# A long convolution and a linear attention in one kernel: paired tail rows, no row of ones, thirds of k, v and q, and a new order

## The chip, the cores and the metric

The kernel runs on one core of a Trainium2 chip. The metric is the device time of one execution in microseconds. Its instructions go to TensorE (matrix products, PE in the profile), VectorE (DVE), ScalarE (ACT), GpSimd (POOL) and SyncE (SP, which issues nearly all DMAs).

## The reference

Two independent computations share the program; their results stand side by side in the output. S = 2048 rows, D = 576 channels, bf16.

```python
# A: a short convolution, a product, a long convolution over the rows, a gate
k_shift = sum(k_pad[:, t:t+S, :] * shift_k[:, 3-t] for t in range(4))
kv = k_shift * v
y = irfft(rfft(pad(kv)) * rfft(pad(ssm_k)))[:, :S] + kv * ssm_D
a = q * y
# B: linear attention, 32 heads of 18 channels
q, k, v = split(x @ wqkv)
phi = lambda t: where(t > 0, t + 1, exp(t)) + 1e-6
kv = einsum("bhsd,bhse->bhde", phi(k), v); z = phi(k).sum(rows)
o = (phi(q) @ kv) / (phi(q) . z + 1e-6)
b = o @ wo
return concatenate([a, b], -1)
```

## The kernel before, in words

A program of some 690 operations is first described (each with the engines it may run on, what it reads and writes) and then issued in one order written out by hand, the text `PLAN`: a letter for the engine (P TensorE, D VectorE, A ScalarE, G GpSimd, S SyncE) and the number of the operation. `PLACES` gives each buffer its address or its PSUM bank. Each engine works through its own operations in that order; semaphores hold an operation until what it reads is there and the buffer that it writes is free. Operations marked `two=1` on GpSimd also wait for the last such operation of VectorE that stands ahead of them in the order, so that products of the two engines run one after the other.

Part A, for three chunks of 192 channels (`CC`):

- `kv_load` loads k (with three rows ahead of each stretch) and v in two halves of 8 rows per partition, all 576 channels in a row. `conv_piece` makes the four taps of a chunk and a half in one product of 6144 columns (`tap`, L423), adds them (`tap+`, once as an accumulating DMA, `acc`, for two of the six pieces) and multiplies by v (`tapv`).
- `h_piece` loads the long filter (`hs`), transposes it on TensorE (`htr`) into hT (`hev`).
- `s1` multiplies by a table (`Gsb`), from hT for the filter (Ch) and from v for the signal (Cu); `s2` transposes in 32 by 32 blocks on VectorE (`tr`, L527) and multiplies by 32 by 32 blocks on TensorE (L538), which gives the spectra sph and spu.
- `inv` multiplies the spectra (`p1`, `p2`, after an exchange X by DMA) and transforms back in part (V; sums `vs` and differences `vd` of its halves); `inv2` does the rest and multiplies by q (`yq`, `i2q`), and `yo` stores.

Part B:

- x comes by DMA, transposed by DMA for three of its four groups of 512 rows (`xT`, `xTt`) and on TensorE for the first (`xtr`, `xev`). 576 is four tiles of 128 rows and one of 64; this last tile is filled up to 128 with rows that meet zeros in the weights and one row of ones (`x4`, `w0`, `w1`, `xo`). The row of ones in x meets a row of ones in the weights and so adds 1 to each product.
- `kproj` (L663): for each of 16 blocks of 128 rows, ten products of 288 columns, then exp(u − 1) on ScalarE (`ek`, L668) and max(min(exp, 1), u) on VectorE (L671), u being the product with 1 added. EPS comes later.
- `qproj` (L685): for each of four groups the query channels in five chunks (`HCH`: four of 126 and one of 72), two, two and one at a time, five products of 512 columns to a chunk, the same phi (L688, L691) into pqT.
- `b_G` (L714) multiplies x by phi(k), with a column of EPS in pk whose result, `gcol`, is added when G is evacuated. From G come kv and z; `den`, `rden` and a pass through memory (`rw`, `rr`) give each query its reciprocal; before that product (`pqn`, L246) a pass on VectorE adds EPS to pqT (`pqe`, L823), and the denominators get their EPS part from 20 products of one column (L785, `dcol`). `b_out` (L860) multiplies by M (kv times wo) and stores.

Many operations pass through helpers: `tt` (L246, products and sums), `copy` (L233 on ScalarE, L235 on VectorE, L237 on GpSimd), `dma` (L226).

Of the kernel before, what the change touches and what calls it, by code (L numbers as in the profile page):

```python
# [16 lines left out]
HALF = 288  # L17
KT = [128, 128, 128, 128, 128]
# [8 lines left out]
EP, WX = True, False  # L27
# [91 lines left out]
def _tables():  # L119
# [69 lines left out]
def kernel(  # L189
# [57 lines left out]

    def psb(banks, name):
        return P.buf(name, [128, banks, 512], FP32, space="ps", banks=banks)
# [16 lines left out]
    wk = SB("wk", [128, 5, D], side=1)  # L266
    wq = SB("wq", [128, 5, D], side=1)
# [3 lines left out]
    pk = [SB("pk%d" % g, [128, 4, D + 1], side=1) for g in range(4)]  # L271
# [10 lines left out]
    hmask = lambda: cs(32, 640).rearrange("p (c m) -> p c m", c=5)  # L282
    maskbd = lambda: cs(672, 126)
    epsc = lambda: cs(798, 1)

    P.op("G", lambda e: nc.gpsimd.memset(neg1.t[:], -1.0), wr=[neg1], name="neg1", ms=1)
    for wx in (wk, wq):
        P.op("G", lambda e, wx=wx: nc.gpsimd.memset(wx.t[0:64, 4, :], 0.0), wr=[(wx, "o")], name="w0", ms=576)
        P.op("G", lambda e, wx=wx: nc.gpsimd.memset(wx.t[0:1, 4, :], 1.0), wr=[(wx, "o")], name="w1", ms=576)
    for g in range(4):  # L290
        P.op("G", lambda e, g=g: nc.gpsimd.memset(x4[g].t[:, :, 0:64], 1.0), wr=[(x4[g], "o")], name="x1", ms=256, st="x1%d" % g)
        P.op("G", lambda e, g=g: nc.gpsimd.memset(pk[g].t[:, :, D:D + 1], EPS), wr=[(pk[g], "e")], name="pke", ms=16, st="pke%d" % g)
    if not EP:
        for f in range(2):
            P.op("G", lambda e, f=f: nc.gpsimd.memset(pqT[f].t[64:128, 4, :], 0.0), wr=[(pqT[f], (4, g)) for g in (2 * f, 2 * f + 1)] + [(pqT[f], "r")], name="pqz", ms=1024, st="pqz%d" % f)
# [4 lines left out]
    load("cst", cst, lambda e: dma(e, cst.t[:], C_d), 256 * Ct.shape[1], 1612)  # L300
# [26 lines left out]
    def x_pairs(g):  # L327
# [8 lines left out]
        for p in range(2):  # L336
            for t0, tn in ((0, 4), (4, 1)):
                ps = psb(1, "xps")

                def tr(e, t0=t0, tn=tn, ps=ps, p=p):  # L340
                    o = ps.t.rearrange("p b c -> p (b c)").bitcast(BF)
                    for j in range(tn):
                        for i in range(2):
                            nc.tensor.transpose(out=o[:, 256 * j + 128 * i:256 * j + 128 * i + 128],
                                                in_=x4[g].t[:, 2 * p + i, :] if t0 == 4 else x_sb[g].t[:, 2 * p + i, 128 * j:128 * j + 128],
                                                identity=ident())
# [4 lines left out]
                P.op("P", tr, rd=[(x4[g], ("m", p)), (x4[g], "o"), idw] if t0 == 4 else [(x_sb[g], p), idw], wr=[ps], name="xtr",  # L351
# [3 lines left out]
    def xt_load(g):  # L355
# [9 lines left out]
        if g in XD:  # L365
# [4 lines left out]
            P.op("G", lambda e: nc.gpsimd.memset(b.t[0:1, 4, :], 1.0), rd=[(b, 4)], wr=[(b, 4)], name="xo", ms=512)  # L370
            return

    def wload(which, key):
        c0 = which * D
        wx = wk if which else wq
        load("wqk" + key, wx, lambda e: dma(e, wx.t[:, 0:4, :], ap(wqkv, c0, [[3 * D, 128], [3 * D * 128, 4], [1, D]])),
             589824, 1152, wr=[(wx, "m")], engs=EARLY)
        load("wqkt" + key, wx, lambda e: dma(e, wx.t[64:128, 4, :], wqkv[512:576, c0:c0 + D]), 73728, 1152,
             wr=[(wx, "t")], engs=EARLY)
# [32 lines left out]
    def conv_piece(cc, bh):
        kh, vt = khs[bh], vs[bh]
# [11 lines left out]
        P.op("D", tap, rd=[kh, (Wj, cc)], wr=[(m, 0), (m, 2)], name="tap",  # L425
# [5 lines left out]
        else:  # L431
# [4 lines left out]
        P.op("DG", lambda e: tt(e, vt.t[:, :, c0:c0 + CC], m.t[:, 0], vt.t[:, :, c0:c0 + CC], ALU.mult),  # L436
             rd=[(m, 0), (vt, "v")], wr=[(vt, cc)], name="tapv", n=1536, x2=1, two=1, st=st)
# [38 lines left out]
    def s1(cc, nm):  # L476
        dt = nm == "h" and cc in HDT
        C = SB("C" + nm, [128, CC // 4, 4, 32] if dt else [128, CC // 2, 32, 2])
        for ri in range(2):
            for bg in range(4):  # L480
                ps = psb(2, "s1ps")

                def mm(e, ri=ri, bg=bg, ps=ps):
                    for j in range(4):
                        b = 4 * bg + j
                        src = hT[cc].t[:, b, :] if nm == "h" else vs[bg // 2].t[:, b % 8, CC * cc:CC * cc + CC]
# [12 lines left out]
                rdk = [(vs[bg // 2], cc)] if nm == "u" else [(hT[cc], (i, bg // 2)) for i in range(5) if HP[i] < CC * cc + CC and HP[i + 1] > CC * cc]  # L499
# [7 lines left out]
    def s2(C, cc, pp, nm):  # L507
# [38 lines left out]
        if nm == "h":  # L546
# [55 lines left out]
    def inv2(gi):  # L602
# [4 lines left out]
        nb = 512 // n  # L607
        for bg in range(16 // nb):
# [11 lines left out]
            if ya:  # L620
# [5 lines left out]
                def mul2(e, bg=bg, yb=yb):  # L626
                    qs = qb.t[:, nb * (bg - 1):nb * (bg + 1), c0:c0 + n]
                    return tt(e, qs, yb.t[:], qs, ALU.mult)
                if bg % 2:
                    P.op("DG", mul2, rd=[yb, (qb, "q")], wr=[(qb, (gi, bg - 1)), (qb, (gi, bg))], name="yq", n=2 * nb * n, x2=1, two=1, st=st)  # L630
            elif bg % 2:
# [3 lines left out]
                def mul1(e, bg=bg, yb=yb):  # L635
                    qs = qb.t[:, nb * bg:nb * bg + nb, c0:c0 + n]
                    return tt(e, qs, yb.t[:], qs, ALU.mult)
                P.op("DG", mul1, rd=[yb, (qb, "q")], wr=[(qb, (gi, bg))], name="yq", n=nb * n, x2=1, two=1, st=st)
            else:
                def mul(e, bg=bg, yv=yv):  # L640
                    qs = qb.t[:, nb * bg:nb * bg + nb, c0:c0 + n]
                    tt(e, qs, yv(), qs, ALU.mult)
                P.op("D", mul, rd=[ps, (qb, "q")], wr=[(qb, (gi, bg))], name="i2q", n=nb * n, st=st)
            ns = max(nb, 4) if ya or gi not in YA else nb
            if (bg + 1) * nb % ns == 0:
# [3 lines left out]
                    qb.t[:, b4:b4 + ns, c0:c0 + n]), 256 * ns * n, 2 * n,  # L649
                     rd=[(qb, (gi, kk)) for kk in range(b4 // nb, (b4 + ns) // nb)], wr=[])  # L650
# [3 lines left out]
    def kproj(r):  # L654
        ps = psb(2, "kps")
        eb = SB("ek", [128, 2, HALF])
# [3 lines left out]
        def mm(e):  # L660
            for hh in range(2):
                for t in range(5):
                    nc.tensor.matmul(ps.t[:, hh, 0:HALF],  # L663
                                     lhsT=cols(xT.t[0:KT[t], t, :], r),
                                     rhs=wk.t[0:KT[t], t, HALF * hh:HALF * hh + HALF],
                                     start=(t == 0), stop=(t == 4))
        P.op("P", mm, rd=[wk] + ([xT] if r // 4 in XD else [(xT, (r % 4 // 2, t0)) for t0 in (0, 4)]), wr=[ps], name="k", mm=[(288, 128, 128)] * 10, st=st)
        P.op("A", lambda e: nc.scalar.activation(  # L668
            out=eb.t[:], in_=ps.t[:, :, 0:HALF], func=ACTF.Exp, bias=neg1.t[:]), rd=[ps, neg1], wr=[eb], name="kexp",
             n=576, st=st)  # L670
        P.op("D", lambda e: nc.vector.scalar_tensor_tensor(  # L671
            out=pk[r // 4].t[:, r % 4, 0:D].rearrange("p (h c) -> p h c", h=2), in0=eb.t[:], scalar=1.0,
            in1=ps.t[:, :, 0:HALF], op0=ALU.min, op1=ALU.max), rd=[ps, eb, (pk[r // 4], "e")], wr=[(pk[r // 4], r)], name="kphi", n=576, st=st)

    def qproj(c0, m, g):
# [6 lines left out]
        def mm(e):  # L682
            for c in range(c0, c0 + m):
                for t in range(5):
                    nc.tensor.matmul(ps.t[0:hn, c - c0, :], lhsT=wq.t[0:KT[t], t, HCH[c][0]:HCH[c][0] + hn], rhs=xT.t[0:KT[t], t, :],  # L685
# [308 lines left out]
```

## Time and profile before

| | |
|---|---|
| runs | 161.87, 162.35, 163.82 us; median 162.35 |
| profiled execution | 160.18 us; its span in the profile 158.4 us |
| TensorE busy | 143.7 us (91%) |
| VectorE busy | 141.2 us (89%) |
| ScalarE busy | 128.4 us (81%) |
| GpSimd busy | 55.6 us (35%) |
| DMA | 34.21 MB in 26237 packets, 15786 of them under 512 B |

The profile is of one execution. Busy time of TensorE is the time in which at least one product is under way. A row of a group reads: line, engine, operation, what is written from what, shapes, count, then busy us and the mean ns of one, then the engine's idle time just before them and what ended it. A stretch row gives for each engine busy us and the count of its instructions. Timeline rows are start, length, engine, line, operation.

### The profile page before, as it was taken

Reading aid. Unit: us, or ns where it says so; the run is one execution under the profiler, and the core shown is the slowest. Engines: PE = TensorE matmul, PEld = TensorE weight load, DVE = VectorE, ACT = ScalarE, POOL = GpSimd, SP = SyncE. Lnnn points to the kernel's source line nnn. Section 1 sums busy time; section 2 is a strip of 40 time slices with the busy share of each in tenths; the row PEclk is TensorE's granted clock in tenths of the full one; section 3 lists DMA queues with packets and bytes.
Section 4 is the critical chain, followed back from the end, with each engine's and each line's share of the span. In section 5 each row is a group of like instructions: output and inputs, shape, how many; then the busy total and the mean of one; then the engine's idle time right before and its main releaser. Section 6 shows DMA issues by size and latency. Waiting matters only on the chain.

```text
span 158.4 us, 4045 instructions
## 1 busy us (share of the span) xinstructions
PE 143.7 (91%) x1653; PEld 110.8 (70%) x1653; DVE 141.2 (89%) x161; ACT 128.4 (81%) x181; POOL 55.6 (35%) x48
## 2 busy tenths in 40 slices
PE   6799899999999999999999996877999999989860
PEld 2479676567785789677888885545567788889750
DVE  1245999999999999998999969999999999999980
ACT  3048889989977957744789999799999999998860
POOL 8300310012555789037903553999300000004020
PEclk9999999999999999999999999999999999999998
DMA  4999199999804997179337982799468707952975
GB/s 116 341 405 305 10 244 276 334 199 320 183 0 138 347 262 311 31 270 176 90 107 183 255 209 91 274 333 357 126 271 304 263 2 261 390 177 78 258 198 143
DMA packets 26237, 34.21 MB, mean 216 GB/s; under 512 B 15786, under 2 KB 20907, under 8 KB 25450
## 3 DMA queue, kind: packets, MB, share of 16 engines
q1 hardware_dynamic: 25674, 32.37, 65.4%
q0 software_dynamic: 544, 1.57, 5.5%
q8 instruction: 13, 0.21, 0.6%
q14 instruction: 6, 0.05, 0.1%
HBM read 20.70 MB, written 4.99 MB: 162 GB/s over the span
## 4 chain that ended last, share of the span: by engine, by line
DVE 43%; PE 26%; DMA 16%; issue 6%; ACT 6%; SPq 1%; DVEq 0%; ACTq 0%
PE ps_all L685 8%; PE ps_all L663 7%; DMA m<-m 7%; DVE X L246 6%; DMA kh<-in_A_k_dram 5%; DVE sph L246 5%; DVE m L423 4%; PE ps_all L714 4%; DVE ct L527 4%; DMA wk<-in_B_wqkv_dram 4%; DVE V L246 3%; DVE spu L235 3%; DVE m L246 3%; DVE VS L246 3%; PE ps_all L488 3%
## 5 line engine op out<-in xcount | busy, mean ns | idle before, releaser
L685 PE MATMUL ps_all<-xT,wq 128*126 128x512 bf16 (+1 forms) x100 | 23.4, 379 | 0.4 <-DVE pqT L691 0.2
L860 PE MATMUL ps_all<-M,pqT 126*128 126x288 bf16 (+1 forms) x160 | 21.9, 286 | 1.4 <-ACT M L233 0.7
L663 PE MATMUL ps_all<-wk,xT 128*128 128x288 bf16 x160 | 21.1, 286 | 0.8 <-DMA wk<-in_B_wqkv_dram 0.8
L246 POOL TENSOR_TENSOR pqT<-pqT,rb 126x1024 bf16<-126x1024 bf16 (+1 forms) x9 | 18.9, 2129 | 7.6 <-DVE pqT L823 4.2
L860 PEld LDWEIGHTS <-pqT 126*128 126x128 bf16 (+1 forms) x160 | 17.1, 110 | 4.9 <-issue 1.6
L233 ACT ACTIVATE Cu<-ps_all 128x768 bf16<-128x768 f32 x23 | 18.7, 856 | 2.1 <-DVE den L796 0.9
L423 DVE TENSOR_TENSOR m<-kh,Wj 128x6144 bf16<-128x6144 bf16 x6 | 20.0, 3351 | 0.0
L663 PEld LDWEIGHTS <-xT 128*128 128x128 bf16 x160 | 17.2, 110 | 3.9 <-DVE xT L235 0.8
L488 PEld LDWEIGHTS <-Gsb 128*128 128x128 bf16 x192 | 16.0, 97 | 4.8 <-issue 2.3
L233 ACT ACTIVATE Ch<-ps_all 128x768 bf16<-128x768 f32 x19 | 15.4, 845 | 4.2 <-PE ps_all L488 4.0
L233 ACT ACTIVATE V<-ps_all 128x1024 bf16<-128x1024 f32 x18 | 18.1, 1103 | 0.4 <-PE ps_all L576 0.4
L685 PEld LDWEIGHTS <-wq 128*126 128x126 bf16 (+1 forms) x100 | 12.8, 131 | 7.8 <-issue 1.1
L233 ACT ACTIVATE sph<-ps_all 128x1024 bf16<-128x1024 f32 x16 | 16.0, 1032 | 2.2 <-PE ps_all L538 2.2
L246 POOL TENSOR_TENSOR m<-m 128x3072 bf16<-128x3072 bf16 (+1 forms) x3 | 15.1, 5049 | 6.8 <-ACT eq L688 5.4
L714 PE MATMUL ps_all<-pk,x_sb 128*128 128x288 bf16 (+1 forms) x128 | 17.1, 286 | 0.0
L668 ACT ACTIVATE ek<-ps_all,neg 128x576 bf16<-128x576 f32 x16 | 11.9, 742 | 5.1 <-PE ps_all L663 4.7
L246 POOL TENSOR_TENSOR q<-yb,q 128x768 bf16<-128x768 bf16 (+1 forms) x2 | 2.5, 1275 | 36.8 <-DVE V L246 30.5
L714 PEld LDWEIGHTS <-x_sb 128*128 128x128 bf16 x128 | 12.3, 98 | 2.9
L233 ACT ACTIVATE spu<-ps_all 128x1024 bf16<-128x1024 f32 x14 | 14.1, 1090 | 0.0
L671 DVE SCALAR_TENSOR_TENSOR pk<-ek,ps_all 128x576 bf16<-128x576 bf16 x16 | 11.7, 750 | 1.9 <-ACT ek L668 1.9
L688 ACT ACTIVATE eq<-ps_all,neg 126x1024 bf16<-126x1024 f32 (+1 forms) x12 | 11.6, 972 | 2.1 <-PE ps_all L685 2.1
L691 DVE SCALAR_TENSOR_TENSOR pqT<-eq,ps_all 126x1024 bf16<-126x1024 bf16 (+1 forms) x12 | 12.0, 1027 | 0.0
(88 smaller groups left out, 294.5 us busy)
## 6 DMA issues: line engine op xcount, KB each, us to landing
X<-sph SPq DMA_DIRECT2D x18, 256.0 KB
v<-in_A_v_dram SPq DMA_DIRECT2D x2, 1152.0 KB
out_dram<-ob SPq DMA_DIRECT2D x16, 144.0 KB
q<-in_A_q_dram SPq DMA_DIRECT2D x1, 2304.0 KB
out_dram<-q SPq DMA_DIRECT2D x11, 192.0 KB
rb<-r_scr SPq DMA_DIRECT2D x8, 252.0 KB
x_sb<-in_B_x_dram SPq DMA_DIRECT2D x3, 576.0 KB
kh<-in_A_k_dram SPq DMA_DIRECT2D x1, 1584.0 KB
```

The costliest lines, as they stand in the source:

```text
L233: nc.scalar.activation(out=o, in_=i, func=ACTF.Copy)
L246: return (nc.vector if e == "DVE" else nc.gpsimd).tensor_tensor(out=o, in0=a, in1=b, op=op)
L423: return nc.vector.tensor_tensor(out=m.t[:], in0=i0, in1=i1, op=ALU.mult)
L488: nc.tensor.matmul(ps.t[:, bank, lo - 384 * bank:hi - 384 * bank], lhsT=Gsb.t[:, b, ri, :], rhs=src[:, lo - CC * j:hi - CC * j], start=Tru ...
L663: nc.tensor.matmul(ps.t[:, hh, 0:HALF], lhsT=cols(xT.t[0:KT[t], t, :], r), rhs=wk.t[0:KT[t], t, HALF * hh:HALF * hh + HALF], start=(t == 0 ...
L668: P.op("A", lambda e: nc.scalar.activation(out=eb.t[:], in_=ps.t[:, :, 0:HALF], func=ACTF.Exp, bias=neg1.t[:]), rd=[ps, neg1], wr=[eb], na ...
L671: P.op("D", lambda e: nc.vector.scalar_tensor_tensor(out=pk[r // 4].t[:, r % 4, 0:D].rearrange("p (h c) -> p h c", h=2), in0=eb.t[:], scal ...
L685: nc.tensor.matmul(ps.t[0:hn, c - c0, :], lhsT=wq.t[0:KT[t], t, HCH[c][0]:HCH[c][0] + hn], rhs=xT.t[0:KT[t], t, :], start=(t == 0), stop=( ...
L688: P.op("A", lambda e: nc.scalar.activation(out=eb.t[0:hn], in_=ps.t[0:hn], func=ACTF.Exp, bias=neg1.t[0:hn, :]), rd=[ps, neg1], wr=[eb], n ...
L691: P.op("D", lambda e: nc.vector.scalar_tensor_tensor(out=pqT[g // 2].t[0:hn, c0:c0 + m, 512 * (g % 2):512 * (g % 2) + 512], in0=eb.t[0:hn] ...
L714: nc.tensor.matmul(ps.t[0:m, 0, 0:n], lhsT=x4[r // 4].t[:, r % 4, :] if t == 4 else x_sb[r // 4].t[:, r % 4, 128 * t:128 * t + 128], rhs=p ...
L860: nc.tensor.matmul(ps.t[:, hh - h, 0:HALF], lhsT=cols(pqT[r // 8].t[0:128 if c == 4 and not EP else hn, c, 512 * (r // 4 % 2):512 * (r // ...
```

## The change

- **Tails in pairs.** The last tile of x's rows is held twice, on partitions 0 to 63 and 64 to 127. `kproj` does eight products over four full tiles and then one tail product for each half of its columns, the first on partitions 0 to 63, the second on 64 to 127, into two PSUM banks. `qproj` does the same for its two chunks.
- **No row of ones.** exp(u) is taken without a bias; a new operation (`kmin`, `qmin`: `cap1`, on GpSimd or VectorE) makes min(exp, 1) + EPS; phi is max(u + 1 + EPS, that). The passes that add EPS to pqT, the EPS column of pk, gcol, dcol and its 20 products, and the memsets of w0 and w1 go.
- **Last query columns with the keys.** The last 72 query channels are computed by `kproj` as its first 72 columns (324 columns a half for 288, `KH`), and `qtail` transposes them from pk on TensorE (four transposes a group) and copies them into pqT. The fifth chunk of `qproj` goes.
- **k, v, q by 192 channels.** Each chunk of 192 channels has its own k, v and q tile, loaded in pieces of 8 rows per partition; a row in memory is then 384 bytes.
- **New order.** `PLAN` and `PLACES` are written anew. It begins with the filter (hs, htr, s1 for Ch) and has the key blocks after it. Of the 24 new caps 16 are on GpSimd and 8 on VectorE. The additions of taps that were GpSimd's (two long, one short) are VectorE's, five more of the products with the reciprocal too; five sums and differences of V are GpSimd's; two more evacuations of spectra, two of xT and, net, two of yb are ScalarE's, as are the four copies of the transposed query columns.

```diff
+QT = 72
+KH = 324
...
+    def cap1(e, t):
+        return (nc.vector if e == "DVE" else nc.gpsimd).tensor_scalar(out=t, in0=t, scalar1=1.0, scalar2=EPS, op0=ALU.min, op1=ALU.add)
...
-            P.op("G", lambda e: nc.gpsimd.memset(b.t[0:1, 4, :], 1.0), rd=[(b, 4)], wr=[(b, 4)], name="xo", ms=512)
+            P.op("GDA", lambda e: copy(e, b.t[0:64, 4, :], b.t[64:128, 4, :]), rd=[(b, 4)], wr=[(b, 4)], name="xo", n=512)
...
+        kh = SB("kh%d" % cc, [128, 19, CC])
+        vt = SB("v%d" % cc, [128, 16, CC])
...
+        for bh in range(2):
+            load("kh", kh, lambda e, bh=bh: dma(e, kh.t[:, 3 + 8 * bh:11 + 8 * bh, :], ap(k, 8 * bh * D + c0, [[16 * D, 128], [D, 8], [1, CC]])),
+                 2048 * CC, 2 * CC, wr=[(kh, "m%d" % bh)])
...
         def mm(e):
             for hh in range(2):
-                for t in range(5):
-                    nc.tensor.matmul(ps.t[:, hh, 0:HALF],
-                                     lhsT=cols(xT.t[0:KT[t], t, :], r),
-                                     rhs=wk.t[0:KT[t], t, HALF * hh:HALF * hh + HALF],
-                                     start=(t == 0), stop=(t == 4))
+                for t in range(4):
+                    nc.tensor.matmul(ps.t[:, hh, 0:KH], lhsT=cols(xT.t[:, t, :], r),
+                                     rhs=wk.t[:, t, KH * hh:KH * hh + KH], start=(t == 0), stop=False)
+            for hh in range(2):
+                h = slice(64 * hh, 64 * hh + 64)
+                nc.tensor.matmul(ps.t[:, hh, 0:KH], lhsT=cols(xT.t[h, 4, :], r), rhs=wk.t[h, 4, 0:KH], start=False, stop=True)
...
-            out=eb.t[:], in_=ps.t[:, :, 0:HALF], func=ACTF.Exp, bias=neg1.t[:]), rd=[ps, neg1], wr=[eb], name="kexp",
-             n=576, st=st)
+            out=eb.t[:], in_=ps.t[:, :, 0:KH], func=ACTF.Exp), rd=[ps], wr=[eb], name="kexp", n=2 * KH, st=st)
+        P.op("GD", lambda e: cap1(e, eb.t[:]), rd=[eb], wr=[eb], name="kmin", n=2 * KH, two=1, st=st)
         P.op("D", lambda e: nc.vector.scalar_tensor_tensor(
-            out=pk[r // 4].t[:, r % 4, 0:D].rearrange("p (h c) -> p h c", h=2), in0=eb.t[:], scalar=1.0,
-            in1=ps.t[:, :, 0:HALF], op0=ALU.min, op1=ALU.max), rd=[ps, eb, (pk[r // 4], "e")], wr=[(pk[r // 4], r)], name="kphi", n=576, st=st)
+            out=pk[r // 4].t[:, r % 4, 0:2 * KH].rearrange("p (h c) -> p h c", h=2), in0=ps.t[:, :, 0:KH], scalar=1.0 + EPS,
+            in1=eb.t[:], op0=ALU.add, op1=ALU.max), rd=[ps, eb], wr=[(pk[r // 4], r)], name="kphi", n=2 * KH, st=st)
...
+    def qtail(g):
...
+            for a in range(4):
+                nc.tensor.transpose(out=o[0:QT, 128 * a:128 * a + 128], in_=pk[g].t[:, a, 0:QT], identity=ident())
...
+        P.op("DA", ev, rd=[ps], wr=[(pqT[g // 2], (4, g))], name="qtev", n=512, st=st)
...
-                P.op("D", lambda e, c=c, hn=hn, f=f: nc.vector.tensor_scalar(
-                    out=pqT[f].t[0:hn, c, :], in0=pqT[f].t[0:hn, c, :], scalar1=EPS, scalar2=None, op0=ALU.add),
-                     wr=[(pqT[f], (c, g)) for g in (2 * f, 2 * f + 1)], name="pqe", n=1024, two=1)
```

More of the change, by code (lines that the diff above doesn't have):

```diff
@@ L270 @@
     x4 = [SB("x4%d" % g, [128, 4, 128], side=1) for g in range(4)]
-    pk = [SB("pk%d" % g, [128, 4, D + 1], side=1) for g in range(4)]
+    pk = [SB("pk%d" % g, [128, 4, 2 * KH], side=1) for g in range(4)]
     pqT = [SB("pqT%d" % f, [128, 5, 1024], side=1) for f in range(2)]
@@ L688, in qproj @@
+            for c in range(c0, c0 + m):
+                h = slice(64 * (c - c0), 64 * (c - c0) + 64)
+                nc.tensor.matmul(ps.t[0:hn, c - c0, :], lhsT=wq.t[h, 4, HCH[c][0]:HCH[c][0] + hn], rhs=xT.t[h, 4, :], start=False, stop=True)
+        P.op("P", mm, rd=[xT, wq], wr=[ps], name="q", mm=[(512, 128, 126)] * (4 * m + 1), st=st)
         P.op("A", lambda e: nc.scalar.activation(
-            out=eb.t[0:hn], in_=ps.t[0:hn], func=ACTF.Exp, bias=neg1.t[0:hn, :]), rd=[ps, neg1], wr=[eb],
+            out=eb.t[0:hn], in_=ps.t[0:hn], func=ACTF.Exp), rd=[ps], wr=[eb],
@@ L690, in qproj @@
              name="qexp", n=512 * m, st=st)
+        P.op("GD", lambda e: cap1(e, eb.t[0:hn]), rd=[eb], wr=[eb], name="qmin", n=512 * m, two=1, st=st)
         P.op("D", lambda e: nc.vector.scalar_tensor_tensor(
-            out=pqT[g // 2].t[0:hn, c0:c0 + m, 512 * (g % 2):512 * (g % 2) + 512], in0=eb.t[0:hn],
-            scalar=1.0, in1=ps.t[0:hn], op0=ALU.min, op1=ALU.max), rd=[ps, eb], wr=[(pqT[g // 2], (c, g)) for c in range(c0, c0 + m)], name="qphi",
+            out=pqT[g // 2].t[0:hn, c0:c0 + m, 512 * (g % 2):512 * (g % 2) + 512], in0=ps.t[0:hn],
+            scalar=1.0 + EPS, in1=eb.t[0:hn], op0=ALU.add, op1=ALU.max), rd=[ps, eb], wr=[(pqT[g // 2], (c, g)) for c in range(c0, c0 + m)], name="qphi",
@@ L698 @@
     for g in range(4):
-        for c, m in ((0, 2), (2, 2), (4, 1)) if MQ else [(c, 1) for c in range(5)]:
-            qproj(c, m, g)
+        for c in (0, 2):
+            qproj(c, 2, g)
+        qtail(g)
     GT = SB("GT", [128, 5, D])
-    gcol = SB("gcol", [128, 5], FP32)
     def b_G(t):
```

273 lines of the change are left out of this document (120 added, 153 removed), and 29 rows, old and new, of the table PLACES.

## The prediction

> **What bounds the kernel now.** First the span, then the stretch view in three pieces (columns: matmul, weight loads, VectorE, ScalarE, GpSimd, each busy us with its count; then clock, DMA share, GB/s).
>
> ```profile
> span 158.4 us, 4045 instructions
> ...
> 0.00:20.00 20.00, 17.01 (x149) 12.48 (x150) 9.65 (x17) 10.43 (x16) 6.10 (x20) 1.00 0.71 233
> 20.00:150.00 130.00, 123.92 (x1474) 95.69 (x1472) 127.38 (x137) 115.40 (x159) 48.59 (x27) 1.00 0.72 216
> 150.00:158.40 8.40, 2.81 (x32) 2.59 (x32) 4.13 (x10) 2.59 (x7) 0.91 (x1) 0.92 0.64 177
> ```
>
> In the 130 us of the middle VectorE idles 2.6, TensorE 6.1, ScalarE 14.6. So two engines bound it together, VectorE first; 10.3 us of VectorE idleness lie in the first 20. A gain must come off VectorE, must not return on TensorE, or must come from the start. Counts below come from numbering the operations in both written-out orders.
>
> **TensorE.** The timeline of its matmuls (start, length, what); starts alone give the pace.
>
> ```profile
> 34.30 0.43 PE L538 MATMUL ps_all<-ct,idw 32*32 32x512 bf16 x16
> 34.66 1.41 PE L663 MATMUL ps_all<-wk,xT 128*128 128x288 bf16 x10
> 35.91 2.32 PE L685 MATMUL ps_all<-xT,wq 128*126 128x512 bf16 x10
> 38.07 1.39 PE L663 MATMUL ps_all<-wk,xT 128*128 128x288 bf16 x10
> 39.30 1.14 PE L457 MATMUL ps_all<-idw,hs 96*128 96x96 bf16 x16
> 40.27 1.39 PE L663 MATMUL ps_all<-wk,xT 128*128 128x288 bf16 x10
> 41.59 0.50 PE L538 MATMUL ps_all<-ct,idw 32*32 32x512 bf16 x16
> 42.02 2.37 PE L685 MATMUL ps_all<-xT,wq 128*126 128x512 bf16 x10
> ```
>
> A key product block takes 1.25 and 1.23 us, say 1.24 for ten of 288 columns, 0.431 ns a column. A query block takes 2.16, or 0.216 for each 512 columns. Sixteen 32-row products of 512 columns take 0.36 and 0.43 from their start to the next one's: they run side by side, so two tails in the two halves of the array should too. But the excursion costs more than one product's 0.216: 0.14 in the first case; in the second 0.21, and the key block ahead of it is 0.08 slower (1.32), 0.29 in all. Call this s, 0 to 0.29 for an excursion into half rows, and take 0.2, near the middle of the two shown.
>
> - Keys: 8 products and a pair, 9 × 324 × 0.431 = 1.255 us, plus s: 16 × (1.255 + 0.2 − 1.24) = +3.4.
> - Queries by two chunks: 9 × 0.216 + 0.2 against 2.16, eight times: −0.1.
> - The four last-chunk products go: 4 × 5 × 0.216 = −4.3.
> - Sixteen transposes of these query columns come, at 0.97 / 16 = 0.061 from the row at 39.30: +1.0.
>
> The sum is 0.0; −4.8 with s = 0, +2.2 with s = 0.29. Were the pairs to run in turn, 16 × 0.14 + 8 × 0.216 = 4.0 more.
>
> **VectorE.** Groups by operation (count, then busy us and mean ns of one).
>
> ```profile
> L823 DVE TENSOR_SCALAR pqT<-pqT 126x1024 bf16<-126x1024 bf16 (+1 forms) x10 | 3.8, 423 | 0.0
> L691 DVE SCALAR_TENSOR_TENSOR pqT<-eq,ps_all 126x1024 bf16<-126x1024 bf16 x8 | 9.4, 1207 | 0.0
> L691 DVE SCALAR_TENSOR_TENSOR pqT<-eq,ps_all 72x512 bf16<-72x512 bf16 x4 | 2.7, 666 | 0.0
> L671 DVE SCALAR_TENSOR_TENSOR pk<-ek,ps_all 128x576 bf16<-128x576 bf16 x16 | 11.7, 750 | 1.9 <-ACT ek L668 1.9
> L246 DVE TENSOR_TENSOR V<-V 128x896 bf16<-128x896 bf16 x9 | 5.5, 623 | 0.2
> L235 DVE CAST spu<-ps_all 128x1024 bf16<-128x1024 f32 x4 | 4.8, 1198 | 0.0
> L235 DVE COPY xT<-ps_all 128x1024 bf16<-128x1024 bf16 (+1 forms) x3 | 1.7, 558 | 4.2 <-PE ps_all L344 4.2
> L235 DVE CAST yb<-ps_all 128x384 bf16<-128x384 f32 x4 | 2.0, 548 | 0.0
> L246 DVE TENSOR_TENSOR m<-m 128x3072 bf16<-128x3072 bf16 x2 | 3.5, 1756 | 0.0
> L246 DVE TENSOR_TENSOR m<-m 128x1536 bf16<-128x1536 bf16 x5 | 4.9, 977 | 1.3 <-DMA m<-m 1.3
> L246 DVE TENSOR_TENSOR pqT<-pqT,rb 126x1024 bf16<-126x1024 bf16 x1 | 0.7, 677 | 0.0
> ```
>
> Off it go the ten passes that add EPS (−3.8), four short phi of the queries (−2.7), five sums and differences of V to GpSimd (−3.1), and to ScalarE two evacuations of a spectrum (−2.4), two of xT (−1.1) and net two of yb (−1.1): −14.2. Onto it come wider key phi: (1207 − 666) / 512 = 1.06 ns a column, 72 more, sixteen times, +1.2; eight of the 24 new cap operations, no dearer than the 423 ns row, +3.4; five more products with the reciprocal, +3.4; two more long tap additions, +3.5; a short one, +1.0: +12.5. The net is −1.7; −2.7 if a cap on fewer columns or with less per-instruction cost takes 0.3. Caps are bounded by 0 and 677 ns, so −5.1 to +0.3.
>
> **ScalarE.** The same view.
>
> ```profile
> L668 ACT ACTIVATE ek<-ps_all,neg 128x576 bf16<-128x576 f32 x16 | 11.9, 742 | 5.1 <-PE ps_all L663 4.7
> L688 ACT ACTIVATE eq<-ps_all,neg 72x512 bf16<-72x512 f32 x4 | 2.7, 681 | 0.6 <-PE ps_all L685 0.6
> L233 ACT ACTIVATE sph<-ps_all 128x1024 bf16<-128x1024 f32 x16 | 16.0, 1032 | 2.2 <-PE ps_all L538 2.2
> L233 ACT ACTIVATE gcol<-ps_all 128x1 f32<-128x1 f32 x5 | 0.9, 173 | 0.7 <-PE ps_all L714 0.7
> L233 ACT ACTIVATE yb<-ps_all 128x384 bf16<-128x384 f32 x15 | 7.0, 521 | 0.8 <-PE ps_all L615 0.8
> ```
>
> Four short exponentials (−2.7) and five gcol (−0.9) go. The wider ones cost 72 × (742 − 681) / 64 = 0.07 each, +1.1; four copies of the transposed query columns by the 512-column row +2.7; the evacuations taken over 2 × 1.03 + 2 × 0.52 + 2 × 0.55 = +4.2, and two copies of x and xT, at about the 521 row, +1.0. Sum +5.4, hidden in its 14.6 us of idleness; were that gone, it would become the third bound. GT's evacuations only lose their bias.
>
> **GpSimd and the added wait.** Every phi now waits for a cap behind the exponential; 16 of the 24 caps are GpSimd's. No row shows one.
>
> ```profile
> L246 POOL TENSOR_TENSOR pqT<-pqT,rb 126x1024 bf16<-126x1024 bf16 x7 | 14.8, 2129 | 7.6 <-DVE pqT L823 4.2 <-DVE pqT L246 3.4
> L288 POOL MEMSET wq<- 64x576 bf16 x1 | 0.6, 567 | 0.0
> ...
> 51.59 3.35 DVE L423 TENSOR_TENSOR m<-kh,Wj 128x6144 bf16<-128x6144 bf16 x1
> ...
> 52.34 2.85 POOL L237 COPY x<-x_sb 128x256 bf16<-128x256 bf16 x1 [1.45 <-DMA x_sb<-in_B_x_dram]
> 62.13 1.47 POOL L237 COPY x<-x_sb 128x256 bf16<-128x256 bf16 x2
> ```
>
> By the memset 0.98 ns a column, by the two-input product 2.08: a key cap takes 0.64 to 1.35, and I take 1.0. Twelve of them and four query caps of up to 2.1 come to 25 us at most; five products (−10.6) leave, and two long tap additions, at 2.08 ns a column 12.8. In a run of blocks GpSimd keeps pace with TensorE's 1.4 us, so the wait shows once, at the first key block: +1.0, or 0 if VectorE has transposes of Ch there, or up to 3 when a cap meets a tap: the copy at 52.34 lasted until that 3.35 us tap was nearly over, two at 62.13 took 1.47 together. Behind a late phi VectorE holds the taps, and behind xo2 (which awaits a transposing DMA) GpSimd holds three caps. The Trainium skill (SBUF — State Buffer, Who interferes with whom) says that a VectorE instruction with two SBUF inputs and a GpSimd one that reads SBUF exclude each other; the copy's rows agree, and by it the wait tends to the 3 us end.
>
> **DMA and the start.** Stretches with long k rows, at the slowest full queue, and with 384-byte rows of output; then the start.
>
> ```profile
> 56.00:62.00 6.00, 6.00 (x49) 5.29 (x47) 5.98 (x8) 3.85 (x5) 5.86 (x1) 1.00 1.05 325
> 74.00:76.00 2.00, 2.00 (x46) 1.74 (x39) 1.59 (x2) 1.63 (x4) 2.00 (x1) 1.00 1.05 168
> 154.00:156.00 2.00, 0.00 (x0) 0.00 (x0) 0.55 (x2) 0.00 (x0) 0.00 (x0) 1.00 1.10 294
> ...
> 0.00:4.00 4.00, 2.53 (x7) 0.88 (x7) 0.76 (x2) 1.49 (x2) 3.47 (x12) 1.00 0.46 116
> 4.00:8.00 4.00, 3.18 (x20) 2.00 (x19) 0.92 (x2) 0.38 (x1) 1.28 (x5) 1.00 1.04 347
> 8.00:12.00 4.00, 4.00 (x40) 3.18 (x38) 1.65 (x3) 1.92 (x4) 0.00 (x0) 1.00 1.03 401
> ...
> 34.58 0.58 SPq L226 DMA_DIRECT2D v<-in_A_v_dram  x1
> ```
>
> k, v and q are 7.1 MB, now in 384-byte rows: 21.8 us of a full queue at 325 GB/s, 24.1 at the output's 294, 42 at 168. I take 294; 2.3 us more vanish in the queue's idle 28%. The seventeen more issues on SP, 0.58 each by the last row, cost nothing while transfers already issued keep the queue busy, and 0.58 each where it has run dry. At the start 0.46 MB are in by 4 us, 1.85 by 8 and 3.45 by 12: the first hs (0.6 MB with the identity) by 4.4, all three and half of Gsb (2.17) by 8.8. The filter's transposes and products so run first, and VectorE has steady copies from about 6 us. It idled 5.0 us before that and 5.3 more up to 20; I allow −2 to +0.5 and take −0.8.
>
> **Sum.** −1.7 (VectorE) + 1.0 (first cap) − 0.8 (start) = −1.5, TensorE 0: 160.18 − 1.5 = 158.7 for the profiled execution. The median of the runs shown stands 1.35% above that execution: 160.8. Under 2%, about what a measurement of this kernel can tell from no change.
>
> **Rivals.**
> - *The pairs are cheap* (s near 0, TensorE −4.8) and the start gives its 2, the wait hidden: −1.7 − 2 = −3.7, with caps at 0.3 us −4.7: 155.5, or 157.6 as a median. For it: sixteen small products in 0.36 us. Against: both excursions cost something. Chance 0.35.
> - *TensorE becomes the bound*: the pairs run in turn at s = 0.29, +6.2; its idle 6.1 can give 2.5, leaving +3.7: 163.9, 166.1 as a median. It decides once key blocks pass about 1.5 us. Against it: the side-by-side rows. Chance 0.12.
> - *The 384-byte loads are slow*: at 168 GB/s each third of k and v (1.57 MB) takes 9.4 us for 4.8. The first third lies in the full queue of the start with nothing to cover it: +5, 165.2, median 167.4. It decides below some 200 GB/s. Against it: 294 outward. The Trainium skill (DMA: Bandwidth & Descriptors, Specifications) wants at least 512 bytes for line rate; no run here shows such loads into SBUF. Chance 0.08.
>
> **How the numbers follow.** The forecast has 0.45; its own range is 159.2 to 164. Faster by over 2% is the first rival, 0.35; slower by over 2% the last two, 0.20. The range from 155.2 (s = 0, caps near nothing) to 167 cuts off less than one in ten at each end.
>
> **What would show it.** Key blocks of nine products 1.4 to 1.5 us apart; VectorE near 139 us busy, ScalarE near 134; caps on GpSimd near 1 us; VectorE over 9.65 us busy in the first 20. I am wrong if VectorE waits for GpSimd in many phi, for k or v, or if ScalarE turns out to be the bound.

## The result, and the profile after

The changed kernel takes **185.45 us** (median of four executions, 185.01 to 187.46); the kernel before took 162.11 beside it. The ratio is 1.148, with a 95% interval of 1.137 to 1.160. The forecast was 160.8, with a range from 155.2 to 167.0: the direction is wrong, and the time lies 18 us outside the range. The profiled execution took 187.46 us, its span is 185.7. The ratios here and below leave out executions that were disturbed, at a lower clock, among them 169.50 us of `caps_vector` and 167.89 of `no_caps`.

First the page of the kernel after: span, busy time of each engine, the slices of the granted TensorE clock, and its groups.

```profile
span 185.7 us, 4040 instructions
...
PE 154.9 (83%) x1633; PEld 107.9 (58%) x1633; DVE 140.1 (75%) x151; ACT 130.8 (70%) x184; POOL 76.4 (41%) x53
...
PEclk9999995589996697899955899999999999999999
...
L246 POOL TENSOR_SCALAR ek<-ek 128x648 bf16<-128x648 bf16 x12 | 28.8, 2401 | 18.6 <-ACT ek L671 15.6
...
L674 DVE SCALAR_TENSOR_TENSOR pk<-ps_all,ek 128x648 bf16<-128x648 f32 x16 | 13.3, 832 | 16.4 <-POOL ek L246 16.0
...
L698 DVE SCALAR_TENSOR_TENSOR pqT<-ps_all,eq 126x1024 bf16<-126x1024 f32 x8 | 9.8, 1225 | 9.6 <-POOL eq L246 9.1
L246 POOL TENSOR_SCALAR eq<-eq 126x1024 bf16<-126x1024 bf16 x4 | 14.5, 3625 | 5.4 <-DVE ek L246 5.2
```

VectorE has 1.1 us less work than before (140.1 against 141.2) in a span that is 27.3 longer, so its idle time grew from 17.2 to 45.6 us, by 28.4. The last column of the two rows of phi (L674, L698) names the cause of most of it: 16.0 and 9.1 us in which VectorE stood before a phi and waited for a cap (min(exp, 1) + EPS, L246) on GpSimd. One such cap takes 2.40 us for a key block and 3.63 us for a query block.

The list of waits of the kernel after gives the same by count (total us, times, longest).

```profile
DVE pk L674 <- POOL ek L246: 16.0, 11, 2.3
DVE pqT L698 <- POOL eq L246: 9.1, 4, 2.7
...
DVE eq L246 <- ACT eq L694: 2.5, 2, 1.4
DVE ek L246 <- ACT ek L671: 1.6, 1, 1.6
```

Fifteen of the sixteen caps on GpSimd made VectorE wait, and the four lines come to 29.2 us. The timeline of the first run of key blocks shows how.

```profile
17.81 1.27 PE L665 MATMUL ps_all<-wk,xT 128*128 128x324 bf16 x8
...
19.02 0.31 PE L669 MATMUL ps_all<-wk,xT 64*128 64x324 bf16 x2
...
19.26 1.27 PE L665 MATMUL ps_all<-wk,xT 128*128 128x324 bf16 x8
...
20.71 1.29 PE L665 MATMUL ps_all<-wk,xT 128*128 128x324 bf16 x8
...
21.15 12.19 POOL L246 TENSOR_SCALAR ek<-ek 128x648 bf16<-128x648 bf16 x5 [3.50 <-ACT ek L671]
...
23.57 0.83 DVE L674 SCALAR_TENSOR_TENSOR pk<-ps_all,ek 128x648 bf16<-128x648 f32 x1 [1.47 <-POOL ek L246]
...
24.45 1.26 PE L665 MATMUL ps_all<-wk,xT 128*128 128x324 bf16 x8 [0.74 <-DVE pk L674]
...
26.02 0.83 DVE L674 SCALAR_TENSOR_TENSOR pk<-ps_all,ek 128x648 bf16<-128x648 f32 x1 [1.62 <-POOL ek L246]
...
28.47 0.83 DVE L674 SCALAR_TENSOR_TENSOR pk<-ps_all,ek 128x648 bf16<-128x648 f32 x1 [1.62 <-POOL ek L246]
...
29.36 2.32 PE L665 MATMUL ps_all<-wk,xT 128*128 128x324 bf16 x8 [2.04 <-DVE pk L674]
```

TensorE makes a key block each 1.45 us (17.81, 19.26, 20.71), as forecast. GpSimd runs five caps back to back in 12.19 us, one each 2.44 us, so it falls behind by about 1 us with every block. From 23.57 on the phi follow at that pace (23.57, 26.02, 28.47), and TensorE, whose PSUM is freed only by phi, waits for them in turn (0.74, then 2.04 us). One of the fifteen waits, of 1.3 us, is owed rather to the rule `two=1`: that key cap (start 58.37) began 1.8 us after its exponential had ended, behind a cap on VectorE that stood ahead of it in the order. The last row above shows a second loss: the same eight products that took 1.27 us take 2.32. The stretch view has the clock of that time (columns as in the prediction; the clock stands behind GpSimd).

```profile
24.00:28.00 4.00, 1.93 (x18) 1.20 (x18) 1.23 (x2) 1.79 (x3) 3.92 (x2) 1.00 1.05 298
28.00:32.00 4.00, 2.65 (x14) 1.12 (x13) 2.82 (x3) 0.40 (x1) 3.84 (x3) 0.51 0.61 67
32.00:36.00 4.00, 2.38 (x25) 1.25 (x24) 2.52 (x4) 2.57 (x3) 1.63 (x2) 0.50 0.27 55
```

TensorE was busy 1.93 of 4 us, and in the next stretches its granted clock is 0.51 and 0.50. The Trainium skill (TensorE: Matmul & The Clock Gate, Part 1: The HAM clock gate) says that an array that is not kept busy is cut back to half rate; the rows agree. So the waits for the caps make some products slower too: TensorE's busy time rose by 11.2 us over the kernel before, with twenty products fewer. How much of the loss the clock makes by itself wasn't separated.

### The profile page after: what moved, and what is told of

It is laid out like the page before. It is cut to its first block, busy times and chain, and to the rows that moved or that the text cites. A ratio compares the mean times of both kernels' runs of the same rounds, so it can differ in the third digit from the quotient of the medians.

```text
span 185.7 us, 4040 instructions
## 1 busy us (share of the span) xinstructions
PE 154.9 (83%) x1633; PEld 107.9 (58%) x1633; DVE 140.1 (75%) x151; ACT 130.8 (70%) x184; POOL 76.4 (41%) x53
## 5 line engine op out<-in xcount | busy, mean ns | idle before, releaser
L246 POOL TENSOR_SCALAR ek<-ek 128x648 bf16<-128x648 bf16 x12 | 28.8, 2401 | 18.6 <-ACT ek L671 15.6
L665 PE MATMUL ps_all<-wk,xT 128*128 128x324 bf16 x128 | 25.1, 349 | 8.1 <-DVE pk L674 4.8
L674 DVE SCALAR_TENSOR_TENSOR pk<-ps_all,ek 128x648 bf16<-128x648 f32 x16 | 13.3, 832 | 16.4 <-POOL ek L246 16.0
L665 PEld LDWEIGHTS <-xT 128*128 128x128 bf16 x128 | 14.3, 118 | 16.5 <-issue 10.4
L671 ACT ACTIVATE ek<-ps_all 128x648 bf16<-128x648 f32 x16 | 11.3, 718 | 16.6 <-PE ps_all L669 16.6
L535 PE MATMUL ps_all<-ct,idw 32*32 32x512 bf16 x288 | 13.4, 445 | 9.1 <-DVE pqT L698 5.7
L688 PE MATMUL ps_all<-xT,wq 128*126 128x512 bf16 x64 | 18.4, 438 | 0.0
L698 DVE SCALAR_TENSOR_TENSOR pqT<-ps_all,eq 126x1024 bf16<-126x1024 f32 x8 | 9.8, 1225 | 9.6 <-POOL eq L246 9.1
L737 PE MATMUL ps_all<-pk,x_sb 128*128 128x288 bf16 x128 | 17.0, 286 | 0.1
L246 POOL TENSOR_SCALAR eq<-eq 126x1024 bf16<-126x1024 bf16 x4 | 14.5, 3625 | 5.4 <-DVE ek L246 5.2
L485 PE MATMUL ps_all<-v,Gsb 128*128 128x192 bf16 x96 | 11.4, 251 | 3.0 <-DVE pk L674 2.3
```

The lines of the kernel that those rows point to most:

```text
L246: return (nc.vector if e == "DVE" else nc.gpsimd).tensor_scalar(out=t, in0=t, scalar1=1.0, scalar2=EPS, op0=ALU.min, op1=ALU.add)
L485: nc.tensor.matmul(ps.t[:, bank, lo - 384 * bank:hi - 384 * bank], lhsT=Gsb.t[:, b, ri, :], rhs=src[:, lo - CC * j:hi - CC * j], start=Tru ...
L535: nc.tensor.matmul(ps.t[32 * j:32 * j + 32, kh - k0, :], lhsT=W2()[32 * kh:32 * kh + 32, :], rhs=ct.t[32 * kh:32 * kh + 32, 8 * j:8 * j + ...
L665: nc.tensor.matmul(ps.t[:, hh, 0:KH], lhsT=cols(xT.t[:, t, :], r), rhs=wk.t[:, t, KH * hh:KH * hh + KH], start=(t == 0), stop=False)
L671: P.op("A", lambda e: nc.scalar.activation(out=eb.t[:], in_=ps.t[:, :, 0:KH], func=ACTF.Exp), rd=[ps], wr=[eb], name="kexp", n=2 * KH, st=st)
L674: P.op("D", lambda e: nc.vector.scalar_tensor_tensor(out=pk[r // 4].t[:, r % 4, 0:2 * KH].rearrange("p (h c) -> p h c", h=2), in0=ps.t[:, ...
```

## The experiments

The theory: the size of the caps on GpSimd, with VectorE and then TensorE waiting behind each, makes the loss. Rivals: the 384-byte rows of k, v and q; the new order or the pairs of tail products; a delay on the way from engine to engine rather than the cap's own length.

**All caps on VectorE** (`caps_vector`). In the written-out order each cap of GpSimd goes to VectorE, directly ahead of its phi. Here and below P, D, A and G stand for the engine of an operation.

```diff
-... A(kexp) ... G(kmin) ... D(kphi)
+... A(kexp) ... D(kmin) D(kphi)
```

> The changed kernel with all 24 caps on VectorE, each directly ahead of its phi; nothing else moves. Theory 1 (a cap takes GpSimd 2.4 us for a key block and 3.6 for a query block, and everything behind a phi waits for it): the 25.1 us in which VectorE waited for a cap go, 12 x 0.32 + 4 x 0.42 = 5.6 us of work come, TensorE's granted clock returns to 0.97 or more; 160 to 168 us. Theory 2 (384-byte loads of k, v and q): 180 us or more. Theory 3 (pairs of tails, with the array's clock down because of them): 180 or more, clock below 0.95.

Measured: 163.26 us, ratio 1.014 (1.003 to 1.026), as theory 1 had it; the profiled span is 161.4, 24.3 us shorter. The page and the groups of this kernel:

```profile
PE 145.1 (90%) x1633; PEld 104.9 (65%) x1633; DVE 144.4 (89%) x167; ACT 130.7 (81%) x184; POOL 35.3 (22%) x37
...
PEclk9999999999999999999999999999999999999998
...
L674 DVE SCALAR_TENSOR_TENSOR pk<-ps_all,ek 128x648 bf16<-128x648 f32 x16 | 13.3, 833 | 1.5
L246 DVE TENSOR_SCALAR ek<-ek 128x648 bf16<-128x648 bf16 x16 | 5.1, 316 | 0.0
L246 DVE TENSOR_SCALAR eq<-eq 126x1024 bf16<-126x1024 bf16 x8 | 3.7, 468 | 0.0
```

The waits are gone, the clock is back though the pairs of tails are all still there, TensorE's busy time falls from 154.9 to 145.1 at the same 1633 products, and VectorE does a cap in 0.32 us where GpSimd took 2.40. Sixteen moved operations return 22 of the 23 us.

**Long rows** (`long_rows`, and `caps_vector_long` on top of the former). k, v and q are read as one run of 3072 bytes for each partition.

```diff
-ap(k, 8 * bh * D + c0, [[16 * D, 128], [D, 8], [1, CC]])
+ap(k, 8 * bh * D, [[16 * D, 128], [1, 8 * CC]])
```

> The changed kernel, but k, v and q are read from memory as 3072 contiguous bytes per partition where it reads eight rows of 384; the tiles in SBUF have the same size and place (part A then works on other channels than it should; the instructions are the same). Theory 1 (caps on GpSimd): within 2% of 185.5 us. Theory 2 (384-byte loads): 175 or less. Theory 3 (pairs): within 2%.

> caps_vector with k, v and q read as 3072 contiguous bytes per partition, as in long_rows. If 384-byte rows cost something now that the caps no longer hide it, 160 us or less for 163.3; if not, 162 to 165.

Measured: 186.14 us against 185.45 with the short rows, and 163.35 against 163.26 (ratios to before 1.159, 1.145 to 1.172, and 1.013, 1.004 to 1.021). The 384-byte rows cost no time that shows, neither where VectorE waits nor where it doesn't. They do keep the DMA queue busy a little longer, 73.3% of the span against 71.5% in the second pair.

**One operation in the cap** (`one_op`). The cap stays on GpSimd, without the addition.

```diff
-tensor_scalar(out=t, in0=t, scalar1=1.0, scalar2=EPS, op0=ALU.min, op1=ALU.add)
+tensor_scalar(out=t, in0=t, scalar1=1.0, scalar2=None, op0=ALU.min)
```

> The changed kernel with a cap of one operation, min alone, on the same engines (EPS is left out of that branch of phi). If GpSimd pays for each of the two operations of a cap, its 2.40 us for 648 columns fall to about 1.3 and the time to 165 to 173 us. If it pays per column whatever the number of operations, 2.4 us and 183 to 187 stay.

Measured: 174.59 us, ratio 1.087 (1.072 to 1.102), a little above the expected 165 to 173. Two of its groups, for the waits:

```profile
L674 DVE SCALAR_TENSOR_TENSOR pk<-ps_all,ek 128x648 bf16<-128x648 f32 x16 | 13.3, 830 | 9.9 <-POOL ek L246 9.6
...
L698 DVE SCALAR_TENSOR_TENSOR pqT<-ps_all,eq 126x1024 bf16<-126x1024 f32 x8 | 9.8, 1225 | 5.7 <-POOL eq L246 5.3
```

The single durations of the caps (shortest, median, longest ns), first of the kernel after, then of `one_op`:

```profile
L246 POOL TENSOR_SCALAR ek<-ek x12: 2372/2372/2707, 21.1 to 82.9; 128x648 bf16<-128x648 bf16 x12
...
L246 POOL TENSOR_SCALAR eq<-eq x4: 3620/3626/3627, 45.5 to 92.3; 126x1024 bf16<-126x1024 bf16 x4
```

```profile
L246 POOL TENSOR_SCALAR ek<-ek x12: 1815/1822/1929, 20.4 to 71.3; 128x648 bf16<-128x648 bf16 x12
...
L246 POOL TENSOR_SCALAR eq<-eq x4: 2756/2759/2767, 39.9 to 79.0; 126x1024 bf16<-126x1024 bf16 x4
```

A key cap became shorter by 0.55 us, less than was expected (1.82 in place of some 1.3), and the time fell by 10.9 us: the order of the work and the handovers between engines are the same in both, so the length of the cap is what counts. Lines through the medians: (3626 − 2372) / 376 = 3.34 ns a column and 0.21 us besides with two operations, (2759 − 1822) / 376 = 2.49 with one. For the caps of 576 columns in the next experiment the first line gives 2.13 us, and their median there is 2.13. Shortest and median agree within 7 ns in all four rows, so most caps have one length, as they would not if VectorE's work held them up.

**The caps alone** (`before_caps`). To the kernel before are added, on GpSimd, caps that change no value, at the same twelve key and four query blocks (the cut shows the key caps).

```diff
+            if r in (1, 2, 3, 4, 7, 8, 9, 11, 12, 13, 14, 15):
+                nc.gpsimd.tensor_scalar(out=eb.t[:], in0=eb.t[:], scalar1=1.0, scalar2=0.0, op0=ALU.min, op1=ALU.add)
```

> The kernel before, with a cap (min with 1, plus 0) on GpSimd between exponential and phi for the same 12 key blocks and 4 query blocks as in the changed kernel; its results stay the same. Theory 1: VectorE waits for caps as in the changed kernel, 12 x 2.4 + 4 x 3.6 = 43 us more on GpSimd, 175 to 190 us. Theories 2 and 3: within 3% of 162.

Measured: 195.79 us, ratio 1.219 (1.205 to 1.233), more than was expected. Two of its waits, and the longest in GpSimd's and VectorE's timelines:

```profile
DVE pk L674 <- POOL ek L671: 21.6, 10, 6.8
DVE pqT L697 <- POOL eq L694: 12.6, 4, 5.4
```

```profile
81.60 5.99 POOL L246 TENSOR_TENSOR m<-m 128x3072 bf16<-128x3072 bf16 x1
87.55 4.23 POOL L671 TENSOR_SCALAR ek<-ek 128x576 bf16<-128x576 bf16 x2
...
89.72 1.42 DVE L674 SCALAR_TENSOR_TENSOR pk<-ek,ps_all 128x576 bf16<-128x576 bf16 x2 [6.83 <-POOL ek L671]
```

The caps alone, without any other part of the change and without the rule `two=1` (which these caps don't have), make the loss, and a larger one (34.2 us of waits): in that order GpSimd has its long tap additions among the blocks, and a cap stands behind one of 5.99 us while VectorE waits 6.83. The new order gave these additions to VectorE.

**Key caps alone on VectorE** (`keys_vector`). As the first experiment, but the four query caps stay on GpSimd.

> The twelve key caps of GpSimd go to VectorE, each directly ahead of its phi; the four query caps stay on GpSimd. Theory (VectorE's waits for the caps are the loss, in proportion): the key caps made 16.0 of 25.1 us of waiting, so 16.0/25.1 of the 22.2 us between the changed kernel (185.45) and all caps on VectorE (163.26) come back, 14 us: 171.3, within 169 to 174; VectorE still waits about 2.3 us four times for a query cap. Rival (the slower TensorE clock is the loss, and any waits that remain keep it down): less than half comes back, 175 or more, and the clock stays below 0.95.

Measured: 172.27 us, ratio 1.062 (1.055 to 1.070).

```profile
DVE pqT L698 <- POOL eq L246: 9.3, 4, 2.7
```

The query caps still cost their 9.3 us of waiting, and the key caps' share comes back as expected. The profiles side by side:

| kernel | span, us | VectorE busy, us | VectorE idle, us | of it, waits for caps, us | mean clock |
|---|---|---|---|---|---|
| caps_vector | 161.4 | 144.4 | 17.0 | 0 | 0.996 |
| keys_vector | 170.6 | 143.1 | 27.5 | 9.3 | 0.954 |
| one_op | 171.8 | 139.9 | 31.9 | 9.6 + 5.3 = 14.9 | 0.963 |
| after | 185.7 | 140.1 | 45.6 | 16.0 + 9.1 = 25.1 | 0.916 |
| before | 158.4 | 141.2 | 17.2 | 0 | 0.996 |
| before_caps | 194.5 | 142.3 | 52.2 | 21.6 + 12.6 = 34.2 | 0.894 |

Against the same kernel without caps on GpSimd (`caps_vector`, or the kernel before for the last row), VectorE idles 10.5, 14.9, 28.6 and 35.0 us longer, for waits of 9.3, 14.9, 25.1 and 34.2: nearly one for one. The spans are longer by 9.2, 10.4, 24.3 and 36.1, because a cap on GpSimd also takes its work off VectorE, 4.5 us in `one_op` and 4.3 in the changed kernel.

**No caps** (`no_caps`, and again as `no_caps_more`). All caps on VectorE as before, but left out.

> caps_vector with the 24 caps left out altogether (phi is then max(exp, u + 1 + EPS), without the min). What is left of the change shows its own worth. If VectorE is what bounds caps_vector, its 144.4 us of work fall by 8.8 and the time to 152 to 156 us. If TensorE with its pairs bounds it, 160 to 164.

> All caps on VectorE, as above, but the 24 caps are left out (exp is not limited to 1 and EPS is missing there). The single look gave a span of 157.2 us against 161.4 with the caps. Theory (the caps cost about half of the 8.2 us they keep VectorE busy, the rest of the change is worth about 1 us): 158 to 161 us and a ratio of 0.98 to 1.0 to the kernel before. Rival (without caps VectorE's saving shows in full): 154 to 156, ratio 0.96.

The first gave 159.02 us in a single execution, between its two ranges. The second: 157.89 us, ratio 0.972 (0.965 to 0.979), between the theory's 158 and 0.98 and the rival's 156 and 0.96, so neither was right. The page:

```profile
PE 143.3 (92%) x1633; PEld 104.2 (67%) x1633; DVE 136.0 (87%) x143; ACT 130.1 (83%) x184; POOL 34.9 (22%) x37
```

VectorE's busy time is 136.0 us, 8.4 under `caps_vector`, and the span 156.3, 5.1 under it: some 60% of the work saved shows. All the rest of the change is thus worth about 4 us (162.24 for the kernel before beside it); the caps, even at the better of the two places tried, take this and more.

**Both tails in one half** (`same_half`, on `caps_vector`). The second tail uses partitions 0 to 63 too, so that the pair can't run side by side.

```diff
-h = slice(64 * hh, 64 * hh + 64)
+h = slice(0, 64)
```

> caps_vector with both tails of each pair taken from partitions 0 to 63 (the second tail then multiplies the wrong weights; sizes and count are the same), so that they cannot run side by side. If the pairs do run side by side, a key pair takes 0.39 us for 0.25 from its start to the next product's and a query pair 0.58 for 0.36, 4.0 us of TensorE in all, and the time rises by 1 to 4 us. If they have been running in turn all along, neither the gaps nor the time change (within 0.5%).

Measured: 164.77 us, ratio 1.021 (1.011 to 1.032). TensorE is busy 147.8 us, 2.7 more than in `caps_vector` and less than the 4.0 expected; whether the time rises too stays open, since the interval overlaps that of `caps_vector` (1.003 to 1.026). Its timeline first, then that of `caps_vector`:

```profile
21.56 0.46 PE L669 MATMUL ps_all<-wk,xT 64*128 64x324 bf16 x2
21.96 1.27 PE L665 MATMUL ps_all<-wk,xT 128*128 128x324 bf16 x8
```

```profile
21.80 0.33 PE L669 MATMUL ps_all<-wk,xT 64*128 64x324 bf16 x2
22.06 1.27 PE L665 MATMUL ps_all<-wk,xT 128*128 128x324 bf16 x8
```

From a pair to the next product it is 0.40 us in one half and 0.26 in two: the pairs do run side by side, and save about what a product of 324 columns takes (0.14).

**Products back to GpSimd** (`give_back`, on `caps_vector`). Two products with the reciprocal and three of the products with q go from VectorE to GpSimd, which now is 78% idle.

> caps_vector with two products with the reciprocal (c 2 and 3 of the second half) and three products with q of the first group moved from VectorE to GpSimd, at their places in the order. By the count VectorE loses 2 x 0.68 + 3 x 0.55 = 3.0 us: 159 to 161 us for 163.3. If products of the two engines hold each other up, or if another engine bounds that stretch, within 1% of caps_vector or slower.

Measured: 168.65 us, ratio 1.045 (1.038 to 1.052), a miss: VectorE's busy time rose from 144.4 to 150.4 instead of falling. The timeline shows where:

```profile
126.19 6.12 POOL L243 TENSOR_TENSOR pqT<-pqT,rb 126x1024 bf16<-126x1024 bf16 x2 [1.34 <-DVE q L243]
127.16 6.23 DVE L243 TENSOR_TENSOR X<-spu,X 128x2048 bf16<-128x2048 bf16 x2
```

Two products of X take VectorE 2.4 us otherwise (1.217 each in `caps_vector`), two of GpSimd's 4.2 (2.122 each there). Beside each other both were held up, VectorE by 3.8 us, GpSimd by 1.9; from 126.19 to 133.39 they took 7.2 us together, more than the 6.7 they would take one after the other. Over the whole kernel the nine products of X cost VectorE 5.2 us more than the 10.9 of `caps_vector`:

```profile
L243 DVE TENSOR_TENSOR X<-spu,X 128x2048 bf16<-128x2048 bf16 x9 | 16.1, 1804 | 0.0
```

**The row of ones again, without caps** (`ones_row`). After each pair of tails comes a pair of products of one row; it adds 1 to the sums, and phi is one pass as in the kernel before.

```diff
+            for hh in range(2):
+                o = ones.t[64 * hh:64 * hh + 1, 4:5]
+                nc.tensor.matmul(ps.t[:, hh, 0:KH], lhsT=o.to_broadcast([1, 128]), rhs=o.to_broadcast([1, KH]), start=False, stop=True)
```

> The changed kernel with no caps at all and with the row of ones back: after each pair of tail products comes a pair of products of one row (ones times ones) that adds 1 to each sum, so exp takes a bias of -1 again and phi is max(min(exp, 1), sum) in one VectorE pass. EPS is left out of phi here; the rest is computed. Theory (the caps are what costs, and TensorE has some room): without caps 157.89 us; a second small product of 324 columns cost 0.15 us after another in the same half and one of 512 columns 0.21, so TensorE gets up to 16 x 0.15 + 8 x 0.21 = 4.1 us more. With both tails in one half 2.7 us of TensorE cost 1.5 us of time, so 4.1 cost 2.3: 160.2, within 158.5 to 162, ratio 0.975 to 1.0. Rival (TensorE is already the bound, its 4.1 us show in full): 162 or more, ratio 1.0.

Measured: 163.80 us, ratio 1.017 (1.011 to 1.023), above the expected 158.5 to 162 and in the rival's range. The page (busy time, then the chain that ended last, by engine) and the timeline:

```profile
PE 149.9 (93%) x1681; PEld 106.7 (66%) x1681; DVE 136.4 (85%) x143; ACT 132.2 (82%) x184; POOL 35.5 (22%) x39
...
PE 68%; DVE 17%; DMA 5%; ACT 3%; issue 3%; SPq 1%; ACTq 0%; DVEq 0%
```

```profile
20.09 0.31 PE L675 MATMUL ps_all<-wk,xT 64*128 64x324 bf16 x2
20.33 0.31 PE L678 MATMUL ps_all<-ones 1*128 1x324 bf16 x2
20.57 1.29 PE L671 MATMUL ps_all<-wk,xT 128*128 128x324 bf16 x8
```

A pair of one row takes 0.24 us, as long as the pair of tails of 64 rows, not the 0.15 that the expectation took from `same_half`. TensorE gets 6.6 us more work (143.3 in `no_caps_more`), VectorE 0.4, ScalarE 2.1, and the span grows by 4.9: most of TensorE's work shows, and TensorE makes up 68% of the span on the last chain, so it is the main bound of this kernel. None of the versions that compute everything beats the kernel before.

## Why the prediction was wrong

- **GpSimd and the added wait: the step that failed.** The prediction took 1.0 us for a key cap within bounds of 0.64 and 1.35 (up to 2.1 for a query cap), "so the wait shows once, at the first key block: +1.0". Measured: 2.37 and 3.63 us, above both bounds, and fifteen waits of 25.1 us together. That GpSimd "keeps pace with TensorE's 1.4 us" failed with it, and the loss of clock behind the waits stood nowhere in the sum. The bounds came from a memset (no input) and from a product of two inputs, and one input with two scalar operations was taken to lie between; on GpSimd it doesn't (3.34 ns a column against 2.08 for the product). The size decided the kind of result too: with a cap of 2.37 us against TensorE's 1.45 GpSimd is the slowest stage of exponential, cap and phi, and every block of a run pays, as the phi 2.45 us apart show. Whether a cap under 1.45 us would have shown only once was not tried; the shortest on GpSimd took 1.82. The Trainium skill (GPSIMD Engine Reference, Engine selection) calls one-input operations on GpSimd roughly line-rate. Here the same cap took it 7.5 times as long as VectorE (2372 against 316 ns), so the measurement decides against it for this operation.
- **GpSimd as the slowest stage** was no rival. "VectorE waits for GpSimd in many phi" stood only among the ways to be wrong, without a price or a chance, and the range had no room for it. The quoted copy at 62.13, 2.9 ns a column, was no hint of it: in `before_caps` two such copies took half of that, so they had been held up, as the prediction read them.

```profile
98.47 0.73 POOL L237 COPY x<-x_sb 128x256 bf16<-128x256 bf16 x2
```

- **VectorE, −1.7:** measured −1.1. The eight caps on it took 322 and 423 ns (0.423 was taken for each), the wider phi 832 (826 forecast). Without any cap the forecast's terms give −1.7 − 3.4 = −5.1; `no_caps_more` has 136.0, which is −5.2.
- **TensorE, 0.0 with s = 0.2:** the blocks stand 1.45 us apart (1.455 forecast), the pairs run side by side. In `caps_vector`, with the clock at 0.996, TensorE is busy 1.4 us longer than in the kernel before; the 11.2 of the changed kernel came with the waits. The rivals on pairs that are cheap and on pairs in turn are both out.
- **ScalarE, +5.4:** measured +2.4. Most of the difference is the exponential, which became shorter without its bias (below). GT's evacuations also went from 508 to 419 ns each without theirs, 0.9 us in all, where the prediction counted nothing.
- **DMA, 2.3 us hidden:** hidden, as the long rows showed; the rival of the slow 384-byte loads is out.
- **The start, −0.8:** VectorE is busy 11.83 us of the first 20 where it was 9.65, as the prediction asked; what this is worth in time wasn't measured alone:

```profile
0.00:20.00 20.00, 16.57 (x161) 12.25 (x162) 11.83 (x18) 13.10 (x20) 4.45 (x16) 1.00 0.94 236
```

Without the caps the sum of the forecast would have been −1.7 − 3.4 − 0.8 = −5.9 in place of −1.5; `no_caps_more` stands 4.35 below the kernel before beside it. So one term carried the miss, the wait for the caps, with the clock that it took along.

## What to carry to other kernels

An operation that a trace doesn't show is not safely bounded by two other kinds of operation on the same engine; where it would stand between two engines of a pipeline, compare even its worst case with the pace of the stage, since above that pace it costs its excess in every block, and here it also left TensorE idle enough to lose its clock. The slack of an idle engine (GpSimd, 35% busy) says nothing of its latency. A pass saved by folding a constant into a product row is lost again if it returns as a pass between exponential and phi: the row of ones rode free in a tail that had to be padded anyway.

## What was not expected of the hardware

- GpSimd's scalar operations on bf16 take 3.34 ns a column with two operations and 2.49 with one, so 0.85 for the second; a copy takes 1.4 (two copies of 256 columns in 0.73 us, above), a product of two inputs 2.08.
- An exponential with a bias read from a tile takes 86 to 92 ns longer than one without, at both widths: 808 against 722 ns for 648 columns and 1113 against 1021 for 1024, the kernel `ones_row` with, `no_caps_more` without:

```profile
L680 ACT ACTIVATE ek<-ps_all,ones 128x648 bf16<-128x648 f32 x16 | 12.9, 808 | 7.1 <-PE ps_all L678 7.1
L706 ACT ACTIVATE eq<-ps_all,ones 126x1024 bf16<-126x1024 f32 x8 | 8.9, 1113 | 3.6 <-PE ps_all L704 3.6
```

```profile
L672 ACT ACTIVATE ek<-ps_all 128x648 bf16<-128x648 f32 x16 | 11.4, 722 | 4.9 <-PE ps_all L670 4.8
L695 ACT ACTIVATE eq<-ps_all 126x1024 bf16<-126x1024 f32 x8 | 8.2, 1021 | 2.5 <-PE ps_all L693 2.5
```

- A pair of products of one row costs TensorE as much as a pair of 64 rows (0.24 us for 324 columns).
- Products of VectorE and GpSimd that overlap can hold up both: 6.23 us for 2.4 and 6.12 for 4.2, in `give_back`.
